# Another order of work in the mixed steps of an attention and mixture-of-experts kernel

## The chip, the cores and the metric

The kernel runs on one core of a Trainium2 chip. Its time is the device time of one execution in microseconds; of several executions the median is told. The engines are TensorE (PE; its weight loads are PEld), VectorE (DVE), ScalarE (ACT), GpSimd (POOL) and SyncE (SP, which here only issues DMAs). Each takes its instructions in the order in which the program lists them.

## The reference

Two layers, one after the other. Attention: `kv` is averaged over 4x4 patches, projected with `w_sr` to 768 keys (values are the same) for each of 4 batches, and 12288 queries of 128 channels per batch attend to them with a softmax. The 49152 output rows then pass a top-1 mixture of 8 experts; a row whose skip score is not positive is passed on as it is.

```python
s = scale * (q @ k.transpose(0, 2, 1)); s = s - s.max(-1, keepdims=True)
a = np.exp(s); a /= a.sum(-1, keepdims=True) + 1e-09
x = (a @ v).reshape(B * S, D)
xc = x[x @ w_skip > 0]; logits = xc @ w_gate; e_idx = np.argmax(logits, axis=1)
h = np.maximum(xc[mask] @ w1[e], 0.0)
y[mask] = gate_w[mask, None] * (h @ w2[e])      # for each expert e
out[do_compute] = xc + y
```

## The kernel before, in words

*Attention.* The queries are cut into 384 tiles of 128 rows. For a tile `scores` (L629 on) makes 128x768 scores in two PSUM banks (`s_ps`, two buffers) from six matmuls, `row_max` (L644) takes the negated row maximum on VectorE, `row_exp` (L649) the exponential on ScalarE. The weights are then split in a high and a low fp16 half: `p_hi` (L657) on ScalarE, `p_lo` (L662) on VectorE, and one transposing DMA from SP turns both. `attend` multiplies the turned tile, six tiles later (`LAG`), with the values, 18 matmuls into one PSUM bank shared by two tiles; after the second of them VectorE makes `rs` and ScalarE scales the rows (L722). Every 12 tiles `route` picks experts for 12 rows per partition, in small steps that run as jobs, and hands 12 row scatters to GpSimd (L194), which writes them to `scr`, the list by expert. In tiles before `FIRST` a third of the chunks is turned by TensorE instead.

*Experts.* A block of 512 rows of `scr` is split in fp16 halves by `x_transpose` (two tiles at a time: ScalarE L283, VectorE L286) and turned by a DMA. `up` (L292) makes one of 8 chunks of the hidden layer: three matmuls of 512 columns, the relu to `h_hi` on ScalarE (L300), the low half `h_lo` on VectorE (L301). `down` (L307) takes 12 matmuls of 128 columns for each of its 8 units a block, all into one bank; `gates` scales the block's gate, `finish` (L317) forms four output tiles on VectorE, and four scatters write them to `out`. From L1096 on a loop with a run-time count does this for all experts in groups of 2048 rows.

*The mixed steps.* The fullest expert's first 6 groups (24 blocks, 192 units of up and 192 of down) are peeled: they run beside the last `LEAD` tiles of attention, from tile `FIRST = NTILE - LEAD` on, two units of up and two of down a step, and the rest in a tail: four steps that end the attention, and then a loop of rounds of one up and one down. A down comes no sooner than five ups after its chunk (`ULAG`). In the mixed steps the sums of down, of attention and of up share four PSUM banks (`acc_ps`); in the tail the ups have four of their own. The weights and the first x blocks of the peeled part are fetched and split in the steps ahead of `FIRST`, counted back from it (`first_step`).

*What sets the order.* `tc.manual_schedule()` keeps each engine's instructions in the order of the Python calls. In a mixed step of before that is: scores of the tile, p_lo of the tile before, its row maximum; up; a row scatter; attention of the tile six back; exp; `rs` and row scaling; up; p_hi; the splitting of queries (`q_hi`, `q_lo`); down; down; another scatter and a step of the jobs. The low half of an up is issued right behind its relu, and the x halves right behind the up's seventh and eighth chunk. `scatter_next` takes one waiting row and lets its scatter wait for the last VectorE instruction noted as `paced["by"]`. In a round of the tail, up and down are each followed by a step of the jobs and a scatter. Once all rows are routed and scattered, `flush` loads the block loop's first weights and rows, and `w_scale` and `split_w1` prepare its weights.

Of the kernel before, what the change touches and what calls it, by code (L numbers as in the profile page):

```python
# [25 lines left out]
def kernel(  # L26
# [36 lines left out]
    NGRP = NTILE // GT  # L63
    XW = C + 10
    LAG = 6
    LEAD = 76
    ULAG = 4
    WARM = 6
    PSL = 11
# [96 lines left out]
    xin = [wp.tile([P, TT, ROW], F32, name=f"xin{s}") for s in range(NST)]  # L166
    x16 = wp.tile([P, 2, TT, C], F16, name="x16")
    xT = [wp.tile([P, 2 * TT, P], F16, name=f"xT{s}") for s in range(NST)]
    h, paced, scr_rows, out_rows, first_p, out_p = {}, {}, [], [], [], []

    def alloc_h(pool):
# [117 lines left out]
        if ts[-1] == TT - 1:  # L289
            nc.sync.dma_start_transpose(xT[s], x16.rearrange("p a t c -> p (a t c)"))  # L290

    def up(s, cs):  # L292
        hi, lo = (xT[s][:, i * TT:(i + 1) * TT, :].rearrange("p t x -> p (t x)") for i in range(2))
        for c in cs:
            sl = slice(c * P, (c + 1) * P)
            ps = alloc["h"]()
            nc.tensor.matmul(ps, w1_hi[:, sl], hi, start=True, stop=False)  # L297
            nc.tensor.matmul(ps, w1_hi[:, sl], lo, start=False, stop=False)  # L298
            nc.tensor.matmul(ps, w1_lo[:, sl], hi, start=False, stop=True)  # L299
            nc.scalar.activation(out=h["hi"][:, c, :], in_=ps, func=AF.Relu)  # L300
            paced["by"] = nc.vector.scalar_tensor_tensor(out=h["lo"][:, c, :], in0=ps, scalar=0.0, in1=h["hi"][:, c, :],  # L301
                                                         op0=ALU.max, op1=ALU.subtract).ins

    TERMS = [(w, x, k) for c in range(FC + WL)
             for w, x, k in ((w2_hi, "hi", c), (w2_hi, "lo", c - DL), (w2_lo, "hi", c - WL)) if 0 <= k < FC]
# [82 lines left out]
    def peel_up():  # L388
        for b in range(LB):
            s = b % NST  # L390
            for c in range(FC):
                up(s, [c])
                if c >= FC - 2:
                    x_transpose((s + 2) % NST, range((c - FC + 2) * 2, (c - FC + 3) * 2))
                yield b, c

    def peel_down():
        for b in range(LB):
            s = b % NST
            n = len(TERMS) // FC  # L400
            for k in range(FC):
                if k == 0:
                    y = acc_ps()
                    ys[:] = [y[:, i * C:(i + 1) * C] for i in range(TT)]
                down(k * n, (k + 1) * n)
                if k == FC // 2:
                    gates(s)
                if k == FC - 1 and b < LB - 1:
                    for _ in finish(s):
                        pass  # L410
                yield b, k
                if k == FC - 1 and b < LB - 1:
                    if b + 4 < LB:
                        load_rows(snaps[1 + (b + 4) // NST], s, first_writes, "scr_first")
                    else:
                        finished.append(s)
# [5 lines left out]
    with ExitStack() as p1:  # L422
# [539 lines left out]
        def unit(kind):  # L962
            if t < FIRST or done[kind] == LB * FC:
                return None
            if kind == "down" and done["up"] < min(done["down"] + ULAG + 1, LB * FC):
                return None
            got = next(peels[kind])
            done[kind] += 1
            if kind == "up" and got[1] % 2 == 0 and PADS:
                write_pads(*PADS.pop(0))  # L970
            return got

        t = -1
        while t < NTILE + 3:
            t += 1
            b, tb = divmod(t, TPB)
            live = t < NTILE
            for now, nxt in ((split_a, next_a), (split_v, next_v), (late_a, next_l)):
                now.extend(nxt)
                nxt.clear()  # L980
            if t == FIRST:
                assert not pools and not preps
                p_kv.close()
                first_p.append(p1.enter_context(tc.tile_pool(name="first_p", bufs=HOLD)))
                fill(p1, "fill5", 64)
                alloc_h(p1.enter_context(tc.tile_pool(name="hp1", bufs=1)))
                alloc["h"] = acc_ps
            if t == NTILE:
                p_s.close()
                ps_up = p1.enter_context(tc.tile_pool(name="ps_up", bufs=4, space=PSUM))  # L990
                alloc["h"] = alloc["w"] = lambda: ps_up.tile([P, ST], F32, name="up_ps")
            av = [u for u in ((t - LAG,) if live else (2 * t - NTILE - LAG, 2 * t - NTILE - LAG + 1)) if 0 <= u < NTILE]
            prev = t - 1 if 0 <= t - 1 < NTILE and chunks(t - 1) < KC else None
            if live:
                scores(t, range(t == 0, 2))
            if t < FIRST:
                for u in av:
                    attend(u)
            if prev is not None:
                p_transpose(prev)  # L1000
            if t - 1 in P16:
                p_lo(t - 1)
            if live:
                row_max(t)
            if t < FIRST:
                run_late(early_a)
                run_late(split_a)
                if prev is not None:
                    p_hi(prev)
                run_late(late_a)  # L1010
                row_exp(t)
                run_late(split_v)
                run_late(early_v)
                if prev is not None:
                    p_lo(prev)
                run_late(early_g)
            else:
                if prev is not None:
                    p_hi(prev)
                    run_late(next_a)  # L1020
                    run_late(late_a)
                    run_late(next_v)
                    p_lo(prev)
                unit("up")
                if live:
                    scatter_next()
                for u in av:
                    attend(u)
                if live:
                    row_exp(t)  # L1030
                run_late(early_v)
                run_late(next_l)
                unit("up")
                if live:
                    p_hi(t)
                run_late(early_a)
                run_late(early_g)
                unit("down")
                if live and len(scr_rows) + len(out_rows) > 2 * TT:
                    scatter_next()  # L1040
            if live:
                if t % GT == 0 and t // GT + RG < NGRP:
                    load_q(t // GT + RG)
                for nb, k, r in KV_T.get(t, ()):
                    load_kv(nb, k, [r])
                if b + 1 < B and tb == PREP_T:
                    preps.append(prep_kv(b + 1))
                if t in PAD_T:
                    write_pads(*PADS.pop(0))
            first_step(FIRST - t)  # L1050
            unit("down")
            ph = t % GT
            if ph == 1 and t // GT + 2 < NGRP:
                q_split(t // GT + 2)
            taken.clear()
            if live:
                scatter_next()
            ranked = run_jobs(ph)
            if not live and (not taken or t >= NTILE + 4):
                scatter_next()  # L1060
            if preps and not ranked and (ph != 0 or tb < LAG):
                if next(preps[0], "end") == "end":
                    preps.pop(0)
            if live and b + 1 < B:
                for nb, k, r in KV_T.get(t - 4, ()):
                    if r == R - 1:
                        pools.append(pool_kv(nb, k))
                if pools and len(taken) < 2 and next(pools[0], "end") == "end":
                    pools.pop(0)
                assert not pools or tb < PREP_T, (t, len(pools))  # L1070
        n_it = scale = None
        while done["down"] < LB * FC:
            for kind in ("up", "down"):
                got = unit(kind)
                run_jobs(None)
                if kind == "up" or scr_rows:
                    scatter_next()
                if not ready and not jobs and not scr_rows:
                    ready.append(True)
                flush()  # L1080
            if loaded:
                if scale is None:
                    n_it = nc.values_load(cumi[0:1, 0:1], min_val=1, max_val=NG)
                    scale, since = w_scale(True), done["down"]
                elif done["down"] > since + 6:
                    next(scale, None)
        assert loaded and not finished and not PADS and next(scale, "end") == "end"
        split_w1()
        while out_rows:
            scatter_next()  # L1090
        first_p.clear()
# [76 lines left out]
```

## Time and profile before

| | us |
|---|---|
| median of 3 runs (1783.56 to 1786.06) | 1785.56 |
| profiled execution | 1784.92 |
| its span, first to last instruction | 1783.0 |
| TensorE busy (modelled) | 1708.5 (96%) |
| VectorE busy | 1531.6 (86%) |
| ScalarE busy | 1250.8 (70%) |
| GpSimd busy | 991.3 (56%) |
| attention-only stage | 28 to 786 |
| mixed stage | 786 to 1181 |
| tail | 1181 to 1263 |
| block loop | 1263 to 1783 |

The stages run one after the other and have different limits, so the shares of the span are means over all four. A matmul's end is modelled; how long TensorE needs is better read from the starts of its instructions.

### The profile page before, as it was taken

The numbers are of one execution on the slowest core, as the hardware profiler recorded it, in microseconds if no ns is written. First come the engines' busy times: TensorE is split into PE (matmuls) and PEld (weight loads), VectorE is DVE, ScalarE is ACT, GpSimd is POOL, SyncE is SP. The second block draws the span as 40 slices with busy tenths as digits, with TensorE's granted clock in tenths as the row PEclk, the third lists the DMA queues.
The fourth block names the chain that finished last, engine by engine and source line by source line (L and its number), as shares of the span: only waits on it lengthen the run. The fifth ranks groups of instructions, "written<-read, shape, count | busy, mean of one in ns | idle before, by whom it ended". The sixth has DMA issues, their size and how long they took to land. (4 is left out here: it accounts for less than half of the span.)

```text
span 1783.0 us, 50794 instructions
## 1 busy us (share of the span) xinstructions
PE 1708.5 (96%) x18637; PEld 1420.0 (80%) x18637; DVE 1531.6 (86%) x3205; ACT 1250.8 (70%) x2361; POOL 991.3 (56%) x1256
## 2 busy tenths in 40 slices
PE   5999999999999999989999999997999999999998
PEld 4999999999999999877777777775677777777776
DVE  7999999999999999987777777777788888888887
ACT  3888888888888888776666666663555566655664
POOL 2278757888678787564544454457633333333333
PEclk9999999999999999999999999999999999999999
DMA  6999999999999999987987666563344333343333
GB/s 209 237 244 200 195 211 235 211 204 178 183 198 214 231 201 216 184 186 195 208 199 171 154 155 154 129 135 106 106 97 105 97 98 96 97 106 96 103 103 85
DMA packets 655825, 291.10 MB, mean 163 GB/s; under 512 B 541856, under 2 KB 605984, under 8 KB 655648
## 3 DMA queue, kind: packets, MB, share of 16 engines
q1 hardware_dynamic: 629104, 241.64, 65.3%
q0 software_dynamic: 21504, 38.43, 6.7%
q10 hardware_dynamic: 5040, 8.72, 1.3%
q8 instruction: 105, 1.72, 0.4%
q14 instruction: 72, 0.59, 0.1%
HBM read 85.36 MB, written 79.72 MB: 93 GB/s over the span
## 5 line engine op out<-in xcount | busy, mean ns | idle before, releaser
L194 POOL DMA_INDIRECT scr<-rows,di x384 | 426.0, 1109 | 247.4 <-DVE nm L646 94.5
L652 ACT ACTIVATE p_sb<-s_ps,nm 128x768 f32<-128x768 f32 x384 | 346.7, 903 | 223.2 <-DVE nm L646 222.3
L646 DVE TENSOR_REDUCE nm<-s_ps 128x1 f32<-128x768 f32 x384 | 365.8, 953 | 16.9 <-PE s_ps L640 15.9
L707 PEld LDWEIGHTS <-pt 128*128 128x128 f16 x5064 | 308.8, 97 | 81.5 <-issue 65.7
L194 POOL DMA_INDIRECT out_dram<-o,xin x196 | 195.0, 995 | 317.9 <-DVE o L320 267.9
L300 ACT ACTIVATE h_hi<-h_ps 128x512 f16<-128x512 f32 x384 | 224.1, 598 | 208.7 <-PE h_ps L299 195.1
L707 PE MATMUL acc_ps<-v_hi,pt 128*128 128x138 f16 x3376 | 347.0, 224 | 10.7 <-ACT rows L722 6.4
L311 PEld LDWEIGHTS <-h_hi 128*128 128x128 f16 x4608 | 295.7, 98 | 39.0 <-issue 6.4
L707 PE MATMUL acc_ps<-v_lo,pt 128*128 128x138 f16 x1688 | 320.7, 223 | 0.0
L638 PE MATMUL s_ps<-k_hi,q_hi 128*128 128x384 f32 x768 | 295.0, 384 | 0.4 <-ACT k_hi L513 0.4
L664 DVE SCALAR_TENSOR_TENSOR p<-p_sb,p 128x512 f16<-128x512 f32 (+1 forms) x384 | 290.6, 757 | 1.4 <-ACT p L660 0.7
L640 PE MATMUL s_ps<-k_hi,q_lo 128*128 128x384 f32 x768 | 260.5, 339 | 0.0
L660 ACT ACTIVATE p<-p_sb 128x512 f16<-128x512 f32 (+1 forms) x384 | 258.5, 673 | 2.4 <-DMA pt<-p 0.2
L639 PE MATMUL s_ps<-k_lo,q_hi 128*128 128x384 f32 x768 | 259.4, 338 | 0.0
L301 DVE SCALAR_TENSOR_TENSOR h_lo<-h_ps,h_hi 128x512 f16<-128x512 f32 x384 | 246.1, 688 | 14.9 <-ACT h_hi L300 13.3
L311 PE MATMUL acc_ps<-w_hi,h_lo 128*128 128x128 f16 x2304 | 223.7, 220 | 0.0
L311 PE MATMUL acc_ps<-w_hi,h_hi 128*128 128x128 f16 x2304 | 211.9, 220 | 1.2 <-DVE h_lo L301 0.4
L311 PE MATMUL acc_ps<-w_lo,h_hi 128*128 128x128 f16 x2304 | 211.7, 220 | 0.0
L301 DVE SCALAR_TENSOR_TENSOR h_lo<-acc_ps,h_hi 128x512 f16<-128x512 f32 x152 | 104.4, 687 | 79.7 <-ACT h_hi L300 79.7
L194 POOL DMA_INDIRECT out_dram<-o,ids x92 | 102.3, 1112 | 100.8 <-DVE x L286 39.0
L311 PEld LDWEIGHTS <-h_lo 128*128 128x128 f16 x2304 | 153.9, 98 | 0.9
L297 PE MATMUL h_ps<-xT,w_hi 128*128 128x512 f16 x384 | 146.2, 381 | 2.9 <-issue 2.7
(195 smaller groups left out, 3228.5 us busy)
## 6 DMA issues: line engine op xcount, KB each, us to landing
q_sb<-in_q_dram SPq DMA_DIRECT2D x96, 256.0 KB
out_dram<-rows SPq DMA_DIRECT2D x96, 256.0 KB
xin<-scr SPq DMA_DIRECT2D x75, 264.0 KB, 2.9
kvt<-in_kv_dram SPq DMA_DIRECT2D x74, 256.0 KB
w_raw<-in_moe_w_dram SPq DMA_DIRECT2D x26, 512.0 KB
scr<-pad ACTq DMA_DIRECT2D x32, 264.0 KB
pt<-p SPq DMA_TRANSPOSE x384
scr<-rows,di POOLq DMA_INDIRECT x384
```

The lines of the kernel that those rows point to most:

```text
L194: ins = nc.gpsimd.indirect_dma_start(out=dst, out_offset=bass.IndirectOffsetOnAxis(ap=ids, axis=0), in_=src, in_offset=None, bounds_check= ...
L300: nc.scalar.activation(out=h["hi"][:, c, :], in_=ps, func=AF.Relu)
L301: paced["by"] = nc.vector.scalar_tensor_tensor(out=h["lo"][:, c, :], in0=ps, scalar=0.0, in1=h["hi"][:, c, :], op0=ALU.max, op1=ALU.subtra ...
L311: nc.tensor.matmul(ys[t], h[x][:, k, t * P:(t + 1) * P], w[:, k, :], start=(i == t == 0), stop=(i == len(TERMS) - 1), skip_group_check=True)
L638: nc.tensor.matmul(s[:, h, :HK], q_hi, k_hi[:, sl], start=True, stop=False)
L639: nc.tensor.matmul(s[:, h, :HK], q_hi, k_lo[:, sl], start=False, stop=False)
L640: nc.tensor.matmul(s[:, h, :HK], q_lo, k_hi[:, sl], start=False, stop=True)
L646: paced["by"] = nc.vector.tensor_reduce(out=NM[t], in_=S_PS[t][:, :, :HK], axis=AX.XY, op=ALU.max, negate=True).ins
L652: nc.scalar.activation(out=P_SB[t], in_=S_PS.pop(t)[:, :, :HK], func=AF.Exp, bias=NM.pop(t))
L660: nc.scalar.activation(out=P16[t][:, 0, :], in_=p_flat(t)[:, 0:n], func=AF.Copy, scale=2.0 ** PEXP)
L664: paced["both"] = nc.vector.scalar_tensor_tensor(out=p16[:, 1, :], in0=p_flat(t)[:, 0:chunks(t) * P], scalar=2.0 ** PEXP, in1=p16[:, 0, :] ...
L707: nc.tensor.matmul(ps[:, j % 2, :], w, v[a][:, k, :], start=(i == 0), stop=(i == len(AVL) - 1))
```

## The change

A mixed step has another order, and there are 68 of them (`LEAD`) in place of 76. The scores of the next tile are made at the step's end, ahead of its last down; the row maximum comes ahead of p_lo; one of the two downs opens the step, and a block's `finish` follows it. exp stands ahead of the first up and p_hi ahead of the second. The low half of an up is put into a list (`lows`) that is run after p_hi for the first and behind the second up for the second. Row scaling, query splitting and the x halves (`split_x`) come after that. In the tail, a round is up, low half, x halves, on even rounds a step of the jobs, a scatter, down, finish, and on odd rounds a second scatter while routed rows wait; `w_scale` goes on every second round, and `split_w1` stands right behind it and the last up.

```diff
-    LEAD = 76
+    LEAD = 68
-    def up(s, cs):
+    def up(s, cs, lows=None):
...
             nc.scalar.activation(out=h["hi"][:, c, :], in_=ps, func=AF.Relu)
-            paced["by"] = nc.vector.scalar_tensor_tensor(out=h["lo"][:, c, :], in0=ps, scalar=0.0, in1=h["hi"][:, c, :],
-                                                         op0=ALU.max, op1=ALU.subtract).ins
+            def low(c=c, ps=ps):
+                paced["by"] = nc.vector.scalar_tensor_tensor(out=h["lo"][:, c, :], in0=ps, scalar=0.0,
+                                                             in1=h["hi"][:, c, :], op0=ALU.max, op1=ALU.subtract).ins
+            if lows is None:
+                low()
+            else:
+                lows.append(low)
...
-                if k == FC - 1 and b < LB - 1:
-                    for _ in finish(s):
-                        pass
                 yield b, k
                 if k == FC - 1 and b < LB - 1:
+                    for _ in finish(s):
+                        pass
+                    yield None
                     if b + 4 < LB:
                         load_rows(snaps[1 + (b + 4) // NST], s, first_writes, "scr_first")
...
+            if kind == "up":
+                if got[1] % 2 == 0 and PADS:
+                    write_pads(*PADS.pop(0))
+                if got[1] >= FC - 2:
+                    c = 2 * (got[1] - FC + 2)
+                    split_x.append(lambda: x_transpose((got[0] + 2) % NST, range(c, c + 2)))
+            elif got[1] == FC - 1 and got[0] < LB - 1:
+                ends_b.append(lambda: next(peels["down"]))
...
-            if live:
+            if live and t <= FIRST:
                 scores(t, range(t == 0, 2))
...
-            if t - 1 in P16:
-                p_lo(t - 1)
             if live:
                 row_max(t)
...
+                elif t - 1 in P16:
+                    p_lo(t - 1)
+                unit("down")
+                run_late(ends_b)
+                if live:
+                    row_exp(t)
+                    scatter_next()
                 unit("up")
-                if live:
-                    scatter_next()
                 for u in av:
                     attend(u)
                 if live:
-                    row_exp(t)
+                    p_hi(t)
+                run_late(lows)
                 run_late(early_v)
+                unit("up")
+                run_late(lows)
                 run_late(next_l)
-                unit("up")
-                if live:
-                    p_hi(t)
                 run_late(early_a)
                 run_late(early_g)
-                unit("down")
+                run_late(split_x)
                 if live and len(scr_rows) + len(out_rows) > 2 * TT:
                     scatter_next()
+                if t + 1 < NTILE:
+                    scores(t + 1)
...
-            for kind in ("up", "down"):
-                got = unit(kind)
+            rounds += 1
+            unit("up")
+            run_late(lows)
+            run_late(split_x)
+            if rounds % 2 == 0:
                 run_jobs(None)
-                if kind == "up" or scr_rows:
-                    scatter_next()
...
+            scatter_next()
+            unit("down")
+            run_late(ends_b)
+            if scr_rows and rounds % 2:
+                scatter_next()
...
+            if scale is not None and rounds > since + 6 and rounds % 2 and next(scale, "end") == "end":
+                since = LB * FC
+            if since == LB * FC == done["up"]:
+                split_w1()
+                since += 1
```

## Rows read from the trace of the kernel before

**Rows 1.** Mixed stage: window, length, busy PE, PEld, DVE, ACT, POOL, clock, DMA, GB/s

```profile
786.00:1181.40 395.40, 374.50 (x4039) 299.43 (x4038) 304.17 (x627) 255.24 (x478) 196.89 (x228) 1.00 0.75 172
```

**Rows 2.** Row maxima of attention-only and mixed tiles: ns min/median/max, first, last start

```profile
L646 DVE TENSOR_REDUCE nm<-s_ps x50: 936/958/958, 483.7 to 600.5; 128x1 f32<-128x768 f32 x50
L646 DVE TENSOR_REDUCE nm<-s_ps x76: 946/952/955, 786.0 to 1181.4; 128x1 f32<-128x768 f32 x76
```

**Rows 3.** Timeline of TensorE in one mixed step: start, length, instruction, tile

```profile
1105.54 0.42 PE L638 MATMUL s_ps<-k_hi,q_hi 128*128 128x384 f32 x1
1106.49 0.34 PE L640 MATMUL s_ps<-k_hi,q_lo 128*128 128x384 f32 x1
1106.89 0.38 PE L297 MATMUL acc_ps<-xT,w_hi 128*128 128x512 f16 x1
1107.54 0.28 PE L707 MATMUL acc_ps<-v_hi,pt 128*128 128x138 f16 x2
1109.27 0.39 PE L311 MATMUL acc_ps<-w_hi,h_hi 128*128 128x128 f16 x4
1110.58 0.42 PE L638 MATMUL s_ps<-k_hi,q_hi 128*128 128x384 f32 x1
```

**Rows 4.** Timeline of the other engines in the mixed stage, idle time before in brackets

```profile
1100.04 0.68 DVE L301 SCALAR_TENSOR_TENSOR h_lo<-acc_ps,h_hi 128x512 f16<-128x512 f32 x1
1100.15 0.90 ACT L652 ACTIVATE p_sb<-s_ps,nm 128x768 f32<-128x768 f32 x1 [1.42 <-DVE nm L646]
1100.63 0.63 DVE L286 SCALAR_TENSOR_TENSOR x<-xin,x 128x128 f16<-128x128 f32 x2
1101.68 0.64 ACT L722 ACTIVATE rows<-acc_ps,rs 128x138 f32<-128x138 f32 x2 [0.62 <-DVE rs L717]
1102.21 0.60 ACT L300 ACTIVATE h_hi<-acc_ps 128x512 f16<-128x512 f32 x1
1102.69 0.70 ACT L283 ACTIVATE x<-xin 128x128 f16<-128x128 f32 x2
1103.27 0.85 ACT L660 ACTIVATE p<-p_sb 128x768 f16<-128x768 f32 x1
1103.81 1.08 POOL L194 DMA_INDIRECT scr<-rows,di  x1 [0.80 <-DVE x L286]
1104.43 0.95 DVE L664 SCALAR_TENSOR_TENSOR p<-p_sb,p 128x768 f16<-128x768 f32 x1
1105.29 0.95 DVE L646 TENSOR_REDUCE nm<-s_ps 128x1 f32<-128x768 f32 x1
1106.28 0.90 ACT L652 ACTIVATE p_sb<-s_ps,nm 128x768 f32<-128x768 f32 x1 [1.41 <-DVE nm L646]
1107.08 0.59 ACT L300 ACTIVATE h_hi<-acc_ps 128x512 f16<-128x512 f32 x1
1107.56 0.84 ACT L660 ACTIVATE p<-p_sb 128x768 f16<-128x768 f32 x1
1107.70 0.69 DVE L301 SCALAR_TENSOR_TENSOR h_lo<-acc_ps,h_hi 128x512 f16<-128x512 f32 x1 [0.86 <-ACT h_hi L300]
1108.29 0.60 ACT L300 ACTIVATE h_hi<-acc_ps 128x512 f16<-128x512 f32 x1
1108.44 0.95 DVE L664 SCALAR_TENSOR_TENSOR p<-p_sb,p 128x768 f16<-128x768 f32 x1
1108.67 1.56 POOL L194 DMA_INDIRECT scr<-rows,di  x1 [0.49 <-DVE g_sc L315]
```

**Rows 5.** Group of the mixed stage, 805 to 1165: busy us, mean ns, idle before

```profile
L320 DVE SCALAR_TENSOR_TENSOR o<-acc_ps,g_sc,xin 128x128 f32<-128x128 f32 x68 | 19.0, 343 | 0.0
```

**Rows 6.** Who TensorE waited for in the tail: us in total, times, longest

```profile
PE up_ps L297 <- DVE h_lo L301: 4.6, 2, 3.7
PE up_ps L794 <- POOL oh_all L756: 2.5, 1, 2.5
PE up_ps L221 <- DVE w_dg L218: 2.4, 1, 2.4
```

More of the change, by code (lines that the diff above doesn't have):

```diff
@@ L168 @@
     xT = [wp.tile([P, 2 * TT, P], F16, name=f"xT{s}") for s in range(NST)]
+    lows = []
     h, paced, scr_rows, out_rows, first_p, out_p = {}, {}, [], [], [], []
@@ L391, in peel_up @@
             for c in range(FC):
-                up(s, [c])
-                if c >= FC - 2:
-                    x_transpose((s + 2) % NST, range((c - FC + 2) * 2, (c - FC + 3) * 2))
+                up(s, [c], lows)
                 yield b, c
@@ L407, in peel_down @@
                     gates(s)
+                yield b, k
                 if k == FC - 1 and b < LB - 1:
@@ L410, in peel_down @@
                         pass
-                yield b, k
-                if k == FC - 1 and b < LB - 1:
+                    yield None
                     if b + 4 < LB:
@@ L968, in unit @@
             done[kind] += 1
-            if kind == "up" and got[1] % 2 == 0 and PADS:
-                write_pads(*PADS.pop(0))
+            if kind == "up":
[6 more added lines that the diff above has]
+                ends_b.append(lambda: next(peels["down"]))
             return got
+        split_x, ends_b = [], []
         t = -1
@@ L1071 @@
         n_it = scale = None
+        since = rounds = 0
         while done["down"] < LB * FC:
-            for kind in ("up", "down"):
-                got = unit(kind)
-                run_jobs(None)
-                if kind == "up" or scr_rows:
-                    scatter_next()
[L1078 to L1088, printed above, removed]
+            rounds += 1
[3 more added lines that the diff above has]
+            if rounds % 2 == 0:
+                run_jobs(None)
+            scatter_next()
[3 more added lines that the diff above has]
+                scatter_next()
+            if not ready and not jobs and not scr_rows:
+                ready.append(True)
+            flush()
+            if loaded and scale is None:
+                n_it = nc.values_load(cumi[0:1, 0:1], min_val=1, max_val=NG)
+                scale, since = w_scale(True), rounds
+            if scale is not None and rounds > since + 6 and rounds % 2 and next(scale, "end") == "end":
[3 more added lines that the diff above has]
+                since += 1
+        assert since > LB * FC and not finished and not PADS
         while out_rows:
```

## The prediction

> **What bounds the kernel now.** I read the stages first. In the mixed stage TensorE is busy 374.5 of 395.4 us and VectorE 304.2 [rows 1]. TensorE's figure is modelled, so I measured its own step from its row starts: scores at 1105.54, first up at 1106.89, attention at 1107.54, first down at 1109.27, next scores at 1110.58, which is 5.04 us [rows 3]. Between the first and the last score matmul lie five intervals in 0.95 us, 0.19 each, so the scores were through at 1106.68 and the up stood 0.21 behind them: TensorE alone needs 4.83 us a step. The steps take more. The row maxima of the 76 mixed tiles start from 786.0 to 1181.4, so 395.4/75 = 5.27 us each, while an attention-only step takes (600.5-483.7)/49 = 2.38 us [rows 2].
>
> Something other than an engine's load sets 5.27, and the rows of two steps show it [rows 4]. ScalarE's exp at 1106.28 waited 1.41 us for VectorE's row maximum of 1105.29; the p_lo of 1108.44 waited for ScalarE's p_hi of 1107.56. So the two engines run a ring. Short turn: p_lo 1104.43, row maximum 0.86 later, exp 0.99 later, relu 0.80, p_hi 0.48, next p_lo 0.88, together 4.01 us. The scores that began at 1105.54 are read only behind the p_lo of 1108.44, from about 1109.3: TensorE runs ahead and later waits for PSUM. Long turn, exp 1100.15 to exp 1106.28, 6.13 us: the row scaling starts 1.53 after exp (it waits for `rs`, which stands on VectorE behind a low half and two x halves), relu 0.53, two x halves 0.48, p_hi 0.58, then 1.16 to p_lo (two routing instructions stand ahead of it), row maximum 0.86, exp 0.99. Whatever stands between the links makes a step long.
>
> **The change part by part.** Phases are (t - FIRST) mod 4; the sum is against the profiled execution's 1784.92 us (span 1783.0 and 1.92 around it), and the median shown is 0.64 more.
>
> *Eight steps fewer.* Eight tiles leave the mixed stage: -8 x 5.27 = -42.2. They become attention-only steps: +8 x 2.38 = +19.1. Their 16 ups and 16 downs go to the tail, where TensorE takes 0.65 for an up (1106.89 to 1107.54) and half of 1.31 for a down (1109.27 to 1110.58, two downs) [rows 3]: 16 x 1.31 = +21.0. Together -2.1. The weight loads, splits and first x tiles are counted back from FIRST and move with it, beside attention-only steps as before.
>
> *The new ring.* In the new step VectorE does row maximum, p_lo of the tile before, (phase 2: the finish of a block), low half 1, `rs`, low half 2, (phase 2: q_lo), (phase 3: four x halves); ScalarE does exp, relu 1, p_hi, relu 2, then row scaling, q_hi, x halves. p_lo now uses a p_hi that is a step old, so the ring is row maximum, exp, relu, p_hi, relu, low half 2, row maximum. Links from rows 4: 0.99 + 0.80 + 0.48 + 0.73 (1107.56 to 1108.29) + 0.62 (1107.08 to 1107.70) + 0.59 (1100.04 to 1100.63) = 4.21. VectorE's own work before low half 2 must fit into the first five links, 3.62: 0.86 + 0.86 + 0.59 = 2.31, with a finish 1.2 more (17 finishes of four o in 19.0 us, 1.12 each [rows 5], and the ids at an estimate of 0.1, since the next instruction starts before such a one ends) = 3.51. It fits. By phase:
> phase 1: the row scaling is behind relu 2, off the ring: 4.21.
> phase 0: g_sc on VectorE. The trace has no such row in the groups; its ends are nothing and one x half, 0.31 (the pair of 1100.63 took 0.63). I take the middle, 0.15: 4.36.
> phase 2: q_lo behind low half 2, 0.6, an estimate: the spacing of a low half, which has the same 128x512 shape [rows 4]: 4.81.
> phase 3: relu 2 starts at 3.00; row scaling 0.48 later, first x pair 0.53, second 0.58, its end 0.70: 5.29, and the last x half on VectorE 0.3 more: 5.6. This is the one step that got longer.
> Sum 19.0 in four steps, 4.74 each. Routing adds 0.1: two such instructions cost 1.16 - 0.88 = 0.28 in the long turn, eight in twelve steps about 1.1. So 4.85, against TensorE's 4.83. Two bounds of one size that alternate don't overlap fully; I take 4.92. The ends are 4.83 and the old 5.27. Gain: 68 x 0.35 = -23.8.
>
> *Waits that go.* With the row scaling right behind relu 2 of the odd step, its PSUM bank is free before the attention of the next even step. I count nothing beside the ring for it, TensorE's waits being the ring's shadow.
>
> *Queues.* The transposing DMA of p_lo is issued on SP 0.86 later in its step; its reader comes five steps on. The x transposes come after the second low half, their ups a block (four steps) later. The x loads of a finished block are issued one down later than the finish, with SP free of others that wait. GpSimd's scatters follow the row maximum or a low half as before. All cost nothing while these leads last; without the lead, SP would hold back the transposes behind a load, about one step, once. Scores issued a step's end early need the s_ps bank of two tiles before, whose exp is long done.
>
> *A lock that would speak against it.* The scatter that is now released by the row maximum starts about when p_lo does. In the trace the scatter of 1108.67, started inside a p_lo, took 1.56 instead of about 1.1, while the p_lo of 1104.43, started inside a scatter that ran from 1103.81 to 1104.89, still took its 0.95 [rows 4]: GpSimd paid. The Trainium skill (SBUF — State Buffer, section "SBUF: two separate sides") says of the port pair that VectorE and GpSimd share that whichever starts first holds it for its whole instruction. By that rule a scatter that gets in first would hold up p_lo. As a mechanism of this kernel: p_lo late by 1.08, the scatter's time, is hidden in three phases (3.62 - 2.31 leaves 1.31) but not in the finish step (3.62 - 3.51 leaves 0.11): 17 steps x 0.97 = +16.5.
>
> *The tail.* Here TensorE waits 4.6 us for low halves behind the table's instructions, 2.5 for GpSimd's routing and 2.4 for the weights' scale [rows 6], 9.5 together, each because jobs are issued twice a round. The change issues them every second round, 2 x 1.31 = 2.6 us apart, and splits w1 five rounds before the end. What is late next is GpSimd, whose queue grows while scatters come at 1.5 a round of 1.31 us; each takes 1.08 or more [rows 4]. So I count 8 of the 9.5: -8. The ends are -10 and +4 (a rival below).
>
> Sum: -2.1 - 23.8 - 8 = -33.9, so 1751.0 for the profiled time and 1751.7 beside the median: 1752.
>
> **The rivals.**
> *The ring doesn't shrink.* If each link costs its whole duration and not the start-to-start, the plain turn is 0.95 + 0.90 + 0.60 + 0.84 + 0.60 + 0.69 = 4.58, and with handovers as between 1107.67 and 1107.70 some 4.7; the four phases then give 4.7, 4.9, 5.4 and 6.2, or 5.3 with no routing. For it: the ring has six links where the old had five, and phase 3 carries everything. Against: all the spacings are read from back-to-back rows. The step stays 5.27, and -2.1 - 8 leaves 1775.
> *GpSimd bounds the tail.* The block loop's first x load waits for the last routed row. Jobs at every second round delay the last twelve rows; if they land after the tail's x transposes want them, TensorE stands. By 24 routed rows (two routings) and some 20 output rows ahead of them (the code lets 24 wait), at 1.08 to 1.4 each, that is 48 to 62 us after the tail's rounds start, against about 38 rounds x 1.31 = 50. Price up to 12, and the 8 aren't lost: 1764.
> *The port:* 1752 + 16.5 = 1768.
> *Slower: the PSUM banks.* A low half now comes after p_hi, so an up's bank is held longer. Of four banks one holds the down sums, one or two the attention output. From the point where less than two are left to the ups, the second up waits for low half 1: exp 0.99, relu 1.79, low half 2.41, done 3.10, up and handover 0.9, relu 2 at 4.0, low half 2 at 4.62, row maximum 5.21. With the extras of the phases ((0.15 + 0.6 + 1.39)/4 = 0.54) a step takes 5.75: 68 x 0.48 = +32.6, and with -2.1 and -8 the time is 1808. Against: the row scaling and the finish free their banks before the step's next attention and first down, so two are left in each phase.
>
> **How the numbers follow.** Forecast 1752 (own range 1742 to 1764, from 4.83 and no loss in the tail to 5.05): 0.66. Ring doesn't shrink 0.13, tail 0.10, port 0.05, banks 0.06. About 0.2%, 3.6 us, can be told from no change. Faster by more than that: 0.66 + 0.10 + 0.05 and most of 0.13, less what neither case names, 0.89; within it 0.03; slower 0.08. The range 1741 to 1776 leaves out the banks and the far ends.
>
> **What would show it.** Right: row maxima in the mixed stage 4.85 to 5.0 apart in a pattern of about 4.2, 4.4, 4.8 and 5.6; TensorE's waits for low halves gone; the attention's wait for row scaling gone; the tail without the waits for oh_all and w_dg. Wrong: TensorE waiting for low halves in each step (banks), p_lo over 1.0 us or late in finish steps (port), the x load at the tail's end late (GpSimd), or steps of 5.27.

## The result and the profile after

The changed kernel takes 1754.98 us (median of 4 runs, 1754.38 to 1756.12), the kernel before 1784.56 beside it (4 runs, 1783.17 to 1786.06): a ratio of 0.9835, 95% interval 0.9818 to 0.9852. The forecast was 1752. The profiled execution has a span of 1752.9, against 1783.0.

The 30.1 us between the two spans lie in four stages. Each stage ends at a row that both traces have: the row maximum of the first mixed tile, that of the last tile, the first up of the block loop, the last instruction.

| stage | before | after | difference | forecast |
|---|---|---|---|---|
| up to the first mixed row maximum | 786.0 | 802.5 | +16.5 | +19.1 |
| mixed steps (75 and 67 intervals) | 395.4 | 327.5 | -67.9 | -66.0 |
| tail | 82.1 | 105.0 | +22.9 | +13.0 |
| block loop | 519.5 | 517.9 | -1.6 | 0 |

(The forecast is split as its terms were: -42.2 and -23.8 in the mixed steps, +21.0 and -8 in the tail.) Three stages came within 3 us of it; the tail is 9.9 worse. The total is off by only 3 because the other three together came out 6.1 better than forecast, which is luck. Most of that, 2.6, lies in the first stage, which ends between 801.5 and 805.3 in the traces of all kernels with 68 mixed steps, so it is no more than the spread of that stage.

**The mixed stage.** The window of the stage (length, busy PE, PEld, DVE, ACT, POOL, granted clock, DMA share, GB/s) and the row maxima (ns min/median/max, first and last start), to be read beside [rows 1] and [rows 2]:

```profile
802.50:1130.10 327.60, 321.91 (x3577) 267.25 (x3576) 275.83 (x559) 221.91 (x424) 179.34 (x200) 1.00 0.81 187
```

```profile
L652 DVE TENSOR_REDUCE nm<-s_ps x68: 940/949/957, 802.5 to 1130.0; 128x1 f32<-128x768 f32 x68
```

TensorE went from 95 to 98% busy, and a step takes (1130.04 - 802.51)/67 = 4.89 us where it took 5.27. VectorE and then ScalarE in phases 2 and 3, which answer to [rows 4] (start, length, instruction, idle time before):

```profile
1028.74 0.95 DVE L652 TENSOR_REDUCE nm<-s_ps 128x1 f32<-128x768 f32 x1
1029.60 0.95 DVE L670 SCALAR_TENSOR_TENSOR p<-p_sb,p 128x768 f16<-128x768 f32 x1
1030.47 1.12 DVE L328 SCALAR_TENSOR_TENSOR o<-acc_ps,g_sc,xin 128x128 f32<-128x128 f32 x4
...
1031.58 1.48 DVE L304 SCALAR_TENSOR_TENSOR h_lo<-acc_ps,h_hi 128x512 f16<-128x512 f32 x2
1032.97 0.68 DVE L630 TENSOR_TENSOR q_lo<-q_sb,q_hi 128x512 fp32r<-128x512 f32 x1
1033.57 0.95 DVE L652 TENSOR_REDUCE nm<-s_ps 128x1 f32<-128x768 f32 x1
1034.43 0.95 DVE L670 SCALAR_TENSOR_TENSOR p<-p_sb,p 128x768 f16<-128x768 f32 x1
1035.97 0.69 DVE L304 SCALAR_TENSOR_TENSOR h_lo<-acc_ps,h_hi 128x512 f16<-128x512 f32 x1 [0.59 <-ACT h_hi L301]
...
1037.19 0.69 DVE L304 SCALAR_TENSOR_TENSOR h_lo<-acc_ps,h_hi 128x512 f16<-128x512 f32 x1 [0.20 <-ACT h_hi L301]
1038.01 1.22 DVE L287 SCALAR_TENSOR_TENSOR x<-xin,x 128x128 f16<-128x128 f32 x4
1039.15 0.95 DVE L652 TENSOR_REDUCE nm<-s_ps 128x1 f32<-128x768 f32 x1
```

```profile
1034.55 0.90 ACT L658 ACTIVATE p_sb<-s_ps,nm 128x768 f32<-128x768 f32 x1 [1.72 <-DVE nm L652]
1035.35 0.59 ACT L301 ACTIVATE h_hi<-acc_ps 128x512 f16<-128x512 f32 x1
1035.83 0.84 ACT L666 ACTIVATE p<-p_sb 128x768 f16<-128x768 f32 x1
1036.56 0.60 ACT L301 ACTIVATE h_hi<-acc_ps 128x512 f16<-128x512 f32 x1
1037.04 0.65 ACT L728 ACTIVATE rows<-acc_ps,rs 128x138 f32<-128x138 f32 x2
1037.56 1.29 ACT L284 ACTIVATE x<-xin 128x128 f16<-128x128 f32 x4
```

The ring of the forecast can be walked here: row maximum 1033.57, exp 1034.55, relu 1035.35, p_hi 1035.83, relu 1036.56, low half 2 1037.19, then in this phase 3 the x halves, and the next row maximum at 1039.15, 5.58 after the first. In phase 2 the two starts are 1028.74 and 1033.57, 4.83 apart. A phase 3 takes 5.58 in one of three rounds only. In the other two it takes 6.04 to 6.37, for there two or three routing instructions stand on VectorE behind the x halves, ahead of the row maximum. p_lo and a block's finish stand in VectorE's wait for the relu, the row scaling behind relu 2.

**The tail.** Who TensorE waited for from 1130 to 1236 (us in total, times, longest), against [rows 6]:

```profile
PE up_ps L298 <- DMA xT<-x: 8.6, 1, 8.6
PE up_ps L298 <- DVE h_lo L304: 2.9, 4, 1.5
PE h_ps L298 <- issue: 1.8, 1, 1.8
PE up_ps L222 <- DVE w_dg L219: 0.2, 1, 0.2
PE up_ps L800 <- POOL oh_all L762: 0.2, 1, 0.2
```

The three old waits, 9.5 together, are down to 3.3. A new one has come, 8.6 us for a turned block of x. It is followed back in three views. TensorE around it:

```profile
1196.41 0.39 PE L319 MATMUL acc_ps<-w_lo,h_hi 128*128 128x128 f16 x4
1205.36 0.61 PE L298 MATMUL up_ps<-xT,w_hi 128*128 128x512 f16 x1 [8.56 <-DMA xT<-x]
1205.76 0.63 PE L299 MATMUL up_ps<-xT,w_hi 128*128 128x512 f16 x1
```

SP's DMA issues in the same time:

```profile
1181.27 1.24 SPq L291 DMA_TRANSPOSE xT<-x  x1
1195.27 0.34 SPq L201 DMA_DIRECT2D xin<-scr  x1
1196.49 0.34 SPq L259 DMA_DIRECT2D w_raw<-in_moe_w_dram  x1
...
1198.90 2.66 SPq L291 DMA_TRANSPOSE xT<-x  x1
```

And VectorE's second pair of the x halves that this transpose turns:

```profile
1189.77 0.60 DVE L287 SCALAR_TENSOR_TENSOR x<-xin,x 128x128 f16<-128x128 f32 x2
```

The x halves were there at 1190.37, and the transpose was issued 8.5 us later. Ahead of it on SP stood the x load of 1195.27, and SP's waits in the tail say what that one waited for:

```profile
SPq L201 <- DMA scr<-rows,di: 37.4, 3, 13.6
```

Three x loads held SP for 37.4 us in all (the one of 1195.27 for 12.5), each until a row scatter of GpSimd had landed. In the program such a load waits for the newest scatter to `scr` that was issued before it, though its own rows were written long ago. GpSimd is late by then: from 1178 on its scatters stand end to end, 1.29 apart:

```profile
1191.53 0.98 POOL L195 DMA_INDIRECT scr<-rows,di  x1 [0.30 <-DMA scr<-rows,di]
1192.82 0.98 POOL L195 DMA_INDIRECT scr<-rows,di  x1 [0.31 <-DMA scr<-rows,di]
```

The wait also cost clock. Behind it TensorE worked at the lower level of 1.2 GHz (granted clock 0.51), with starts 0.42 apart instead of 0.22:

```profile
1205.30:1211.20 5.90, 5.84 (x33) 3.75 (x34) 4.38 (x10) 2.84 (x7) 3.35 (x5) 0.51 0.35 98
```

From 1205.36 to 1210.88 there are thirteen such intervals, each about 0.2 longer, which makes 2.7 us. So the wait and what follows it cost about 11.

### The profile page after: what moved, and what is told of

Read it like the earlier page. It is cut to its first block, busy times and chain, and to the rows that moved or that the text cites. A ratio compares the mean times of both kernels' runs of the same rounds, so it can differ in the third digit from the quotient of the medians.

```text
span 1752.9 us, 50769 instructions
## 1 busy us (share of the span) xinstructions
PE 1694.4 (97%) x18653; PEld 1420.8 (81%) x18653; DVE 1535.5 (88%) x3209; ACT 1245.8 (71%) x2365; POOL 997.6 (57%) x1256
## 5 line engine op out<-in xcount | busy, mean ns | idle before, releaser
L319 PEld LDWEIGHTS <-h_hi 128*128 128x128 f16 x4608 | 291.6, 98 | 33.4 <-issue 12.4
L644 PE MATMUL s_ps<-k_hi,q_hi 128*128 128x384 f32 x768 | 301.3, 392 | 0.4 <-ACT k_hi L519 0.4
L644 PEld LDWEIGHTS s_ps<-k_hi,q_hi 128*128 128x128 f32 x768 | 145.8, 190 | 9.5 <-ACT k_hi L519 0.7
L645 PEld LDWEIGHTS s_ps<-k_lo,q_hi 128*128 128x128 f32 x768 | 146.3, 191 | 2.7
```

What stands on the lines that cost most here:

```text
L319: nc.tensor.matmul(ys[t], h[x][:, k, t * P:(t + 1) * P], w[:, k, :], start=(i == t == 0), stop=(i == len(TERMS) - 1), skip_group_check=True)
L644: nc.tensor.matmul(s[:, h, :HK], q_hi, k_hi[:, sl], start=True, stop=False)
L645: nc.tensor.matmul(s[:, h, :HK], q_hi, k_lo[:, sl], start=False, stop=False)
```

## The experiments

The theory: the mixed steps are set by the ring of VectorE and ScalarE, and the tail lost 11 us to SP. The rivals: TensorE sets the steps; the gain is due to fewer mixed steps; the transpose was late of itself. The stages of all runs, from their traces (us; the mixed step is the mean distance of row maxima):

| kernel | median | ratio to before, 95% | first mixed at | mixed step | tail | loop |
|---|---|---|---|---|---|---|
| before | 1784.56 | 1 | 786.0 | 5.27 | 82.1 | 519.5 |
| changed kernel | 1754.98 | 0.9835 (0.9818 to 0.9852) | 802.5 | 4.89 | 105.0 | 517.9 |
| old_order68 | 1779.31 | 0.9967 (0.9955 to 0.9980) | 804.5 | 5.27 | 103.1 | 517.7 |
| order_only76 | 1759.93 | 0.9853 (0.9837 to 0.9869) | 785.1 | 4.89 | 84.0 | 518.8 |
| old_tail | 1756.13 | 0.9840 (0.9826 to 0.9853) | 803.5 | 4.89 | 105.0 | 518.0 |
| load_free | 1743.06 | 0.9769 (0.9755 to 0.9783) | 802.7 | 4.89 | 93.1 | 517.9 |
| old_tail_free | 1750.70 | 0.9805 (0.9792 to 0.9819) | 802.3 | 4.89 | 100.0 | 518.0 |
| plo_first | 1812.46 | 1.0151 (1.0136 to 1.0167) | 804.0 | 5.75 | 103.1 | 517.8 |
| down_short | 1753.62 | 0.9820 (0.9805 to 0.9835) | 802.8 | 4.89 | 103.9 | 518.0 |
| free_spread | 1742.90 | 0.9764 (0.9750 to 0.9777) | 802.2 | 4.87 | 93.3 | 517.9 |
| free_offring | 1762.88 | 0.9787 (0.9774 to 0.9800) | 803.5 | 4.79 | 115.7 | 519.3 |
| offring_short | 1747.76 | 0.9705 (0.9690 to 0.9720) | 801.5 | 4.60 | 115.0 | 518.6 |
| before_free | 1803.11 | 1.0005 (0.9996 to 1.0014) | 785.2 | 5.27 | 100.5 | 520.5 |
| free_offring_again | 1768.00 | 0.9809 (0.9794 to 0.9823) | 805.3 | 4.80 | 120.7 | 520.6 |

The last four ran on two other chips, where the kernel before takes 1802.4, so they are compared by ratio and by stage.

### One part at a time: old_order68 and order_only76

```diff
 (the kernel before)
-    LEAD = 76
+    LEAD = 68
```

> The kernel before with 68 mixed steps in place of 76 and nothing else. The prediction's first term says -2.1 (-42.2 +19.1 +21.0): 1782.5. If the attention-only steps cost 16.5 in place of 19.1, as between the two traces: 1780. Rival (most of the gain is the smaller number of mixed steps): 1765 or less. Mixed steps stay at 5.27.

The span is 1778.1, 4.9 below that of before: mixed 352.8 in place of 395.4 (-42.6), the stages ahead +18.5, the tail +21.0, which is the forecast's 16 x 1.31 to a tenth, and the loop -1.8. So the first term stands, and the smaller number of mixed steps is about a fifth of the whole gain at most.

```diff
 (the changed kernel with the tail's loop of before)
-    LEAD = 68
+    LEAD = 76
```

> Only the mixed steps' order is new: 76 mixed steps and the tail's rounds of before. Theory (the ring is shorter): steps of 4.89 in place of 5.27, 75 x 0.38 = -28.5 from the kernel before, so 1756, with the same pattern of 4.36, 4.23, 4.83 and 5.58. Rival (the gain comes from fewer mixed steps or from the tail): 1775 to 1785.

Mixed 367.1 in place of 395.4: -28.3 for 75 intervals, 0.38 each, as expected. The order of the mixed steps alone carries nearly the whole gain. The span is 1754.9, 28.1 below that of before, with a tail 1.9 longer; the median is 4 above the expected 1756, in runs that lie between 1755.6 and 1760.3. Their spans lie between 1753.6 and 1755.0, so the excess stands outside the span.

### What holds the step: plo_first and down_short

```diff
+            if prev is None and t - 1 in P16:
+                p_lo(t - 1)
             if live:
                 row_max(t)
```

> The changed kernel with p_lo of the tile before put back ahead of the row maximum. Theory (the ring row maximum, exp, relu, p_hi, relu, low half 2 sets the step): p_lo's 0.86 us now stand between low half 2 and the row maximum, so each turn is 0.86 longer, 4.89 + 0.86 = 5.75 a step, +58 over 67 steps: 1812. Rival (TensorE sets the step, p_lo's place is hidden): 1751 to 1759.

1812.46, and 5.75 a step. The step of phase 2 shows where the time goes in:

```profile
1045.80 0.95 DVE L670 SCALAR_TENSOR_TENSOR p<-p_sb,p 128x768 f16<-128x768 f32 x1
1046.67 0.95 DVE L652 TENSOR_REDUCE nm<-s_ps 128x1 f32<-128x768 f32 x1
...
1051.50 0.95 DVE L670 SCALAR_TENSOR_TENSOR p<-p_sb,p 128x768 f16<-128x768 f32 x1
```

From p_lo to p_lo it is 5.70, the 4.83 of the changed kernel and p_lo's 0.87. The swap of p_lo and the row maximum is worth 58 us by itself, more than the gain: without it the rest of the new order would be slower than before.

```diff
             w, x, k = TERMS[i]
+            if w is w2_lo and first_p and t < NTILE and i < len(TERMS) - 1:
+                continue
...
```

> The changed kernel, leaving out 7 of the 24 terms of down (w2's low half) in the mixed steps: 28 of 96 matmuls a block, 7 a step, 7 x 0.054 = 0.38 us of TensorE a step. Theory (VectorE's and ScalarE's ring sets the step): 4.85 to 4.89 a step, 1752 to 1755. Rival (TensorE sets it): 4.51 a step, 1729. In between if the two bounds take turns: some 0.1 a step, 1748.

The window of the mixed stage:

```profile
802.80:1130.40 327.60, 304.20 (x3131) 243.31 (x3129) 275.91 (x559) 221.89 (x424) 179.51 (x200) 1.00 0.79 187
```

With some 450 matmuls fewer (3131 in the records against 3577) the stage has the same 327.6 us, and the twelve intervals of one routing round agree to 0.01. TensorE at 98% busy was not the bound. It was near it, though: the pair below shows how near.

### The tail: load_free, old_tail, old_tail_free, before_free

```diff
             if group:
                 tc.add_to_no_dep_group(group, ins)
+                tc.declare_no_dep(ins, group="scr", reason="rows read first are complete")
```

> The changed kernel, but the loads of the peeled blocks' rows no longer wait for the newest row scatter (their rows were all written before). Theory (SP held by that load): TensorE's 8.7 us wait for an x transpose in the tail, and about 1.4 us of slow clock behind it, go: 1745, between 1743 and 1748; SP's waits for scatters (40.6 us in the tail) are gone. Rival (the transpose was late of itself, by the x halves or by the DMA queues): 1755 as the changed kernel.

1743.06, 11.9 below the changed kernel, which the shorter tail accounts for (93.1 in place of 105.0). TensorE's waits there, and the tail's window:

```profile
PE up_ps L298 <- DVE h_lo L304: 2.9, 4, 1.5
PE h_ps L298 <- issue: 1.3, 1, 1.3
PE up_ps L222 <- DVE w_dg L219: 0.3, 1, 0.3
PE up_ps L800 <- POOL oh_all L762: 0.2, 1, 0.2
```

```profile
1130.20:1223.20 93.00, 88.38 (x1057) 66.83 (x1053) 72.19 (x195) 48.48 (x102) 60.60 (x72) 1.00 0.45 114
```

SP's waits for scatters in the same stretch:

```profile
SPq L201 <- DMA scr<-rows,di: 3.3, 1, 3.3
```

The wait for xT is gone, the other four are much as they were, the clock stays at 1.00, and SP waits 3.3 us for scatters where it waited 37.4. That settles the cause.

```diff
 (the changed kernel; the tail's rounds as before)
+            for kind in ("up", "down"):
+                got = unit(kind)
...
+                run_jobs(None)
+                if kind == "up" or scr_rows:
+                    scatter_next()
```

> The changed kernel with the tail's rounds of before: a step of the jobs after each up and each down, a scatter after each up and, while routed rows wait, after each down. The mixed stage must stay at 4.89 us a step. By the term of the prediction (the new tail is worth 8 us): 1763. By the comparison of the two traces (the tail gained 3 to 5 us at its three waits and lost 10 at one for an x transpose): 1749 to 1755, since the old tail issues its scatters even closer and its x loads wait as long, but its transposes stand elsewhere in the rounds.

1756.13, 1 above what the comparison of the traces gave and 7 below what the prediction's term gave. Its tail is as long as that of the changed kernel, 105.0, with other waits in it: 4.3 for `w_dg`, 3.0 for `oh_all`, 2.6 for a low half. SP stands 30.0 us at two x loads here:

```profile
SPq L201 <- DMA scr<-rows,di: 30.0, 2, 19.8
```

With both edits (old_tail with the line of load_free):

> The rounds of before in the tail, with x loads that don't wait for the newest scatter; the mixed steps are the new ones. If the new rounds are worth the 8 us of the prediction once SP is free: 1743 + 8 = 1751. If the rounds are worth nothing and all of the tail's loss was SP's: 1743 to 1745.

1750.70, 7.6 above load_free; the tails are 100.0 and 93.1. So the new rounds are worth 7 to 8 us as soon as SP is free, which is the size of the forecast's term, and nothing while it is not. Not all of it is what the term counted: TensorE's waits for low halves, `oh_all` and `w_dg` are 7.3 us in old_tail_free and 3.4 in load_free, 3.9 less. The granted clock of the tail is 0.97 against 1.00, and 0.03 of 100 us, some 3 us by this estimate, is the rest. What SP held back differs: with the old rounds the loop's weights came late (`w_dg`, 4.3, and 1.7 with free loads), with the new rounds a block's x. By the traces, and not by a run of its own, the reason is that jobs at every second round route the last rows later: the loop's weights, which wait until all rows are issued, are loaded at 1196.5 and not at 1177.8, and a third x load fell behind row scatters.

> The kernel before with x loads that don't wait for the newest scatter, and nothing else. In its trace SP stood 17 us at one such load, and TensorE waited for no x transpose. Theory (there the wait had cover, and the changed kernel lost the cover): 1783 to 1786. Rival (the wait cost the kernel before as much, and the comparison of the tails hides it): 1773.

(The same line in the kernel before.) No difference. SP's waits for scatters in the tail of the kernel before:

```profile
SPq L200 <- DMA scr<-rows,di: 27.4, 2, 17.1
```

The 17.1 us are the load of a peeled block, issued at 1220.93, and no one needed what was behind it; the other wait is that of the block loop's own first load, which the line doesn't touch. The tail of this run is 18 us longer than in the first trace of before, at a granted clock of 0.87 in place of 0.94; that is put down to this chip, for the kernel before takes 1802.4 on it as well. The comparison is one within this chip; on the others before_free was not run.

### Room in the ring: free_spread, free_offring, offring_short

```diff
 (load_free)
-                run_late(split_x)
+                if split_x:
+                    split_x.pop(0)()
```

> The version with free x loads (1743), and the two pairs of x halves of a block in two steps, one pair in phase 3 and the other in phase 0 of the next step. By the ring's links phase 3 falls from 5.6 to 5.0 and phase 0 rises from 4.36 to about 4.65, 0.3 less in four steps or 0.07 a step: 1738 if the ring alone sets the time. If TensorE sets it over four steps: 1743, unchanged.

1742.90, as load_free. Phase 3 fell by 0.58 to 0.63, but phase 0 rose by 0.53, not by 0.3:

```profile
1041.15 0.69 DVE L304 SCALAR_TENSOR_TENSOR h_lo<-acc_ps,h_hi 128x512 f16<-128x512 f32 x1 [0.53 <-ACT h_hi L301]
1041.76 0.60 DVE L287 SCALAR_TENSOR_TENSOR x<-xin,x 128x128 f16<-128x128 f32 x2
1042.28 0.22 DVE L323 TENSOR_SCALAR g_sc<-xin,y_sc 128x4 f32<-128x4 f32 x1
```

A pair behind low half 2 costs its own 0.52 in whatever step it stands; spreading moves it and saves nothing. The expectation mis-sized phase 0. TensorE, whose own step is about 4.79 by the next pair, did not eat the gain.

```diff
 (load_free; x_transpose cut into x_high on ScalarE and x_low on VectorE)
                     p_lo(t - 1)
+                if split_d:
+                    split_d.pop(0)()
                 unit("down")
```

> The version with free x loads (1743), and VectorE's two pairs of x halves off the ring: ScalarE's halves stay where they are, VectorE's stand behind p_lo in the next two steps, where VectorE waits 0.59 us for low half 1. The ring alone would then need 4.36, 4.23, 4.83 and 4.23, 4.41 a step, with routing 4.55: 1720 if the ring goes on setting the step. If TensorE's own 4.83 to 4.88 sets it from here: 4.83 to 4.89 a step, 1739 to 1743, with TensorE full. I expect the second.

The same with the shorter down:

> The same kernel, leaving out 7 of the 24 terms of down (w2's low half) in the mixed steps, 0.38 us of TensorE a step. If the ring without the x halves needs 4.55 and TensorE now 4.45 to 4.50: 4.55 to 4.65 a step, 67 x 0.24 to 0.34 below 1743, 1720 to 1727. If the x halves were not what made the ring longer than 4.55: 1743.

Their mixed windows, free_offring first:

```profile
803.50:1124.40 320.90, 318.68 (x3582) 266.28 (x3580) 274.17 (x559) 224.69 (x424) 177.05 (x200) 1.00 0.83 191
```

```profile
801.50:1109.90 308.40, 300.75 (x3131) 242.40 (x3129) 273.66 (x559) 222.38 (x424) 179.71 (x200) 1.00 0.83 197
```

With the x halves in VectorE's wait ahead of low half 1 the step falls to 4.79 with TensorE 99% busy, and to 4.60 once TensorE has less to do. Here, and not in the changed kernel, the same matmuls are worth something: 0.19 a step. So the ring without x halves is about 4.6 (worked out: 4.55), and TensorE's own step about 4.79, a little under the forecast's 4.83.

> The kernel with free x loads and VectorE's x halves off the ring once more, since the third set ran on a chip where the kernel before itself took 1802.4 and its tail was 18 us longer at a lower granted clock. Theory (the mixed stage's 4.79 a step is TensorE's and the rest is as in the version with free loads): 67 x 0.10 = 6.7 below 1743, 1736, ratio to before 0.973, where before takes 1785. Rival (the later x halves cost the tail what the steps win): 1743, ratio 0.9765. On a chip like the third set's: 0.979 again, and nothing is told.

It met such a chip again: 0.9809, with a tail of 120.7 at a granted clock of 0.90. The mixed stage repeats (4.80). Whether the 6.7 us won there reach the total, or the later x halves cost the tail as much, these runs don't tell, since load_free wasn't run on those chips. In the tail of free_offring TensorE waits for no x transpose; what it shows are 12.9 us of pauses of the kind told of at the end. The best version whose total is shown is load_free.

## Why the prediction was right, and where it was not

**Eight steps fewer** (-2.1). Measured alone: -3.1 in the three stages it named (+18.5 -42.6 +21.0), and -1.8 in the loop, which it had at nothing.

**The new ring** (-23.8). The step went from 5.27 to 4.89 where 4.92 was taken. The phases forecast were 4.36, 4.21, 4.81 and 5.6; the ones without routing measured 4.36, 4.23, 4.83 and 5.58. Links read as start-to-start distances in back-to-back rows were right to 0.02, and plo_first, worked out by them before it ran, came out at 1812 as written. Routing adds 0.14 a step, not 0.1, most of it in phase 3 (0.5 and 0.8 in two of three). What was wrong is the remark that two bounds of one size lose something by alternating: the ring alone sets 4.89 (down_short), and TensorE's 4.79 fits under it without a loss. Two readings of the rows of before were off without harm. The trace does have a row of g_sc (L315, 0.22 long), and the next instruction starts 0.13 behind it, near the 0.15 taken. And p_lo of 1108.44 has no idle time ahead of it: VectorE came to it from a low half and g_sc at about the moment at which p_hi ended, so either set it.

**Queues, and the tail** (-8, measured +1.9). The step that failed is the sentence that the x loads of a finished block are issued "with SP free of others that wait" and that all queues cost nothing. In the term of the tail itself the three waits of TensorE fell from 9.5 to 3.3, 6.2 of the forecast's 8. But "what is late next is GpSimd" was followed only to the loop's first x load. GpSimd's queue, in which each scatter takes up 1.29 us and not the 1.08 of the working, came due earlier and in another place: through SP, at the x loads of the peeled blocks, with a transpose behind one of them. 8.6 us of wait and 2.7 of slow clock replaced what was won. The trace of before had shown it: SP stands 17.1 us at such a load in its tail, a row of SP's own waits that the working didn't use. It was costless only by the distance of what stood behind it. With that wait taken away the tail comes out 10.0 below the old order's 103.1, beyond the forecast's 8; the granted clock rose with it, from 0.95 to 1.00, which the term didn't count.

**The rivals.** The ring shrank. TensorE's waits for low halves in the mixed stage fell from 11.4 us to 2.6, and those for the row scaling from 7.1 to 0.2, so the PSUM banks had room. The port: p_lo in the mixed stage (ns min/median/max):

```profile
L670 DVE SCALAR_TENSOR_TENSOR p<-p_sb,p x69: 681/948/953, 801.9 to 1130.9; 128x768 f16<-128x768 f32 x67, 128x512 f16<-128x512 f32 x2
```

Its full-size form has one length, 0.95, with scatters at its side. One p_lo and the two scatters around it:

```profile
1049.01 0.95 DVE L670 SCALAR_TENSOR_TENSOR p<-p_sb,p 128x768 f16<-128x768 f32 x1
```

```profile
1048.35 0.98 POOL L195 DMA_INDIRECT scr<-rows,di  x1 [1.91 <-DVE mx L767]
1049.63 1.18 POOL L195 DMA_INDIRECT scr<-rows,di  x1 [0.30 <-issue]
```

38 full-size p_lo of the mixed stage start while a scatter runs, as this one does. All take 0.95 and start 0.86 or 0.87 behind the row maximum, as the others do. 37 scatters start inside a p_lo, and each ends 0.84 to 0.93 us behind that p_lo's end, however early in it they started; the longest takes 1.60. So in these rows a scatter is held until p_lo is through, and p_lo is not held by a scatter. The Trainium skill's rule (SBUF — State Buffer, "SBUF: two separate sides") that whichever of the two starts first holds the port for its whole instruction agrees with this where p_lo came first, and shows nothing on VectorE where the scatter did. GpSimd did bound the tail, but not by the way and the place that rival named.

**The deferred low halves change nothing by themselves.** This is read off the program; no run was made of it. With the low half issued right at its relu again, every engine's list of instructions in the changed kernel would be the same as with the list `lows`: between the relu and the deferred low half stand only TensorE's and ScalarE's instructions and nothing on VectorE. So the rival of the PSUM banks began from something that the list doesn't do. What the new order moves is p_lo and the row maximum against each other, p_hi, the scaling and the x halves. Of these only the first was measured by itself (58 us); what each of the others is worth stays open.

## What to carry to other kernels

Find the ring of engines that hand a tile to each other and add its links as start-to-start distances: that sum, not an engine's busy share, gives the step, and a TensorE at 98% may still be its shadow. Before a step is moved, read the waits of the queue that issues its DMAs too: a load that waits for the newest of many writes holds everything that the queue issues behind it, and it costs nothing only until something urgent stands there. An edit can earn its full price and not show it: the new tail rounds were worth nothing with SP blocked and 7 us with it free.

## What the hardware showed beside

The tail is not the same on all chips for one program. On the chip of before_free the order of before has 15 pauses in its tail between matmuls of one group, 13.1 us in all and the longest 1.9, for which the trace names no releaser; the first trace of before has none of them. Behind the first eight of them, from 1235.15 on, TensorE's starts lie 0.43 apart and not 0.22, so it had fallen to the lower of its two levels. The tail as a whole had a granted clock of 0.87 in place of 0.94 and was 18 us longer, while the mixed stage kept 1.00. Why that chip pauses is not shown. Scatters that queue on GpSimd start 1.29 us apart, 0.98 each and 0.30 between two, also where the profile names no wait ahead of them.
